# The minimum of 23 ELU blocks moves to GpSimd, and their relu passes go, in a fused attention and FFN kernel

## The chip, the core and the metric

The kernel runs on one core of a Trainium2 chip. The core has TensorE (PE, matmuls, with a queue for weight loads, PEld), VectorE (DVE), ScalarE (ACT), GpSimd (POOL) and SyncE (SP), which issues DMAs. Each engine works through its own instructions in the order in which the program gives them, and waits on semaphores for the others. GpSimd is used on SBUF alone in this kernel; PSUM is read by VectorE and ScalarE. The metric is the device time of one execution in microseconds. Two executions of the kernel before took 331.69 and 332.18 us, median 331.94 us.

## The reference

Attention over 8 batches, 8 heads, 576 queries and 16 "beacon" keys and values ahead of the 576 causal ones, head size 64; its output, 4608 tokens of 512 features, goes through an FFN with an ELU:

```python
scores = scale * np.matmul(q, k_all.transpose(0, 1, 3, 2))   # causal mask but for the beacons
a = np.exp(scores - scores.max(-1, keepdims=True)); a /= a.sum(-1, keepdims=True) + 1e-09
x = np.matmul(a, v_all)               # then to (4608, 512)
h = x @ w_in                          # 512 -> 2048
g = np.where(h > 0.0, h, 1.0 * (np.exp(np.minimum(h, 0.0)) - 1.0))
out = g @ w_out                       # 2048 -> 512
```

The inputs and the output are float32; the kernel works in 16-bit types with float32 sums.

## The kernel before

The tokens are cut into tiles, numbered 0 to 9: two of 256 tokens, then eight of 512. Attention runs by batch (0 to 7), the FFN by tile, interleaved. The whole program is one list of short words, written out by hand in several lines of text (the last argument of `run`); each word calls one step, and the order of the words is the order of the instructions on each engine. The tile framework adds the semaphores and takes buffers from pools in that same order. So a word may be moved only with all that it does on its engine.

The words that matter here, `t` being the tile and `i` a block of 512 PSUM columns:

- `F.t.i` (line 508): FFN1 of one block, four matmuls of 128x512 into a PSUM bank. The banks with the tag "hps" are two, and every F takes the older of them.
- `e.t.i` (line 518): ScalarE's exp of the bank into an SBUF tile "e" (float32, three buffers).
- `u.t.i` (line 524 on ScalarE; with `.v`, line 526 on VectorE): relu of the bank into an SBUF tile "r" (f16, three buffers).
- `k.t.i` (line 536): VectorE's min(exp - 1, relu) from the two SBUF tiles into the FFN2 operand "gt". For a positive h this is h, for a negative one exp(h) - 1.
- `r.t.i` (line 543) and `g.t.i` (line 548): the other form of the same ELU. `r` makes min(exp, 1) - 1 from the SBUF tile "e" into "r", and `g` takes max(h, r) with h read from the PSUM bank. There is no relu. The bank is released only by `g`.
- `Q.t.a.b` (line 624): steps a to b of the 112 matmuls of 128x256 of a tile's FFN2, a Strassen-like scheme of 7 phases of 16; `Z` (line 578) makes the sums of "gt" that it needs, `J` (lines 633 to 640) takes its results from PSUM (the ones on VectorE read PSUM and an SBUF tile) and stores them from SyncE's queue.
- `S`, `x`, `m`, `D`, `L`, `n`, `W`, `M`: a batch's scores (line 317), exp (332), causal mask on VectorE (337), partial sums of the exponentials on VectorE (390), row sums, their reciprocals on ScalarE, the product with v (374), and the scaling that makes the FFN's input (468).
- `P`, `K`, `E`, `U`, `V`, `X`, `H`: in tiles 8 and 9, 12 of the 16 blocks of FFN1 go through another Strassen-like scheme. `P` (line 694) are its matmuls, of 128x256, in the same two "hps" banks.
- `lk`, `lt`, `lp`, `lv`: loads; `lk` and `lv` are DMAs issued by GpSimd, `lp` are small copies on GpSimd.

In the kernel before eight blocks take the form `r`, `g`, with `r` on VectorE: seven in tile 6 and block 7.7. The others take `u` and `k`.

Of the kernel before, what the change touches and what calls it, by code (L numbers as in the profile page):

```python
# [17 lines left out]
def kernel(  # L18
# [519 lines left out]
    op["k"] = kk  # L538

    @step  # L540
    def r(t, i):
# [1 line left out]
        nc.vector.tensor_scalar(
            out=rb[t, i], in0=eb[t, i], scalar1=1.0, scalar2=1.0, op0=ALU.min, op1=ALU.subtract)

    @step
# [307 lines left out]
    m.5.3.1 F.5.10 x.6.8 F.5.5 D.5.3.1 Q.4.35.42 e.5.10 Q.4.42.49 u.5.5 J.4.2 S.6.9 S.6.10 e.5.5
    u.5.10.v k.5.10 Q.4.49.56 D.5.3.2 Z.4.4.1 x.6.10 F.5.8 u.5.8 D.5.2.0 Q.4.56.63 D.5.3.3 x.6.9
    F.5.3 m.6.1.0 S.6.6 Z.4.4.0 e.5.8 lt.7.0 x.6.6 D.5.2.1 k.5.14 D.5.2.2 W.5.1 D.5.2.3 k.5.8
    L.5.1 u.5.3 e.5.3 Q.4.63.70 lp.7.0 F.5.0 k.5.3 m.6.1.1 F.5.4 n.5.1 k.5.5 m.6.0.1 e.5.0
    Q.4.70.77 u.5.0 M.5.1.1 F.5.1 M.5.1.0 e.5.4 u.5.4 D.6.1.0 lp.7.1 J.4.3.v F.5.2 S.6.11 k.5.4
    S.6.12 D.6.0.0 u.5.1 Q.4.77.84 m.6.2.1 J.4.4 Q.4.84.91 e.5.1 k.5.1 D.6.0.1 x.6.12 x.6.11
    u.5.2 Q.4.91.98 D.6.1.1 S.7.4 k.5.0 S.7.2 e.5.2 Z.5.3.1 D.6.1.2 x.7.2 F.5.13 D.6.0.2 k.5.2  # L860
    D.6.1.3 Q.4.98.105 x.7.4 F.5.6 S.7.3 e.5.13 u.5.13 S.6.7 Q.4.105.112 u.5.6 x.7.3 e.5.6 x.6.7
    J.4.5 F.6.2 k.5.13 J.4.6.v e.6.2 D.6.0.3 u.6.2 W.6.0 lv.7 L.6.0 n.6.0 F.6.5 e.6.5 m.6.3.0
    k.5.6 m.6.2.0 u.6.5 m.6.3.1 Z.5.3.0 Z.5.1.0 F.6.3 e.6.3 u.6.3 D.6.2.0 Q.5.0.7 Q.5.7.14
    M.6.0.0 D.6.2.1 F.6.8 M.6.0.1 k.6.3 e.6.8 D.6.2.2 S.7.12 S.7.1 k.6.5 r.6.8 F.6.6 x.7.1
    x.7.12 e.6.6 g.6.8 Q.5.14.21 Z.5.1.1 Z.5.2.0 F.6.9 S.7.0 S.7.5 r.6.6 e.6.9 r.6.9 J.5.0 g.6.6
    D.6.3.0 D.6.2.3 g.6.9 x.7.0 k.6.2 m.7.0.0 Q.5.21.28 Q.5.28.35 J.5.1 x.7.5 F.6.0 Z.5.2.1
    S.7.11 D.6.3.1 u.6.0 e.6.0 S.7.6 F.6.13 F.6.14 D.6.3.2 x.7.6 W.6.1 e.6.13 x.7.11 r.6.13
    D.6.3.3 g.6.13 e.6.14 m.7.1.0 L.6.1 r.6.14 F.6.7 e.6.7 m.7.0.1 u.6.7 D.7.0.0 Q.5.35.42
    Q.5.42.49 F.6.12 D.7.0.1 n.6.1 g.6.14 e.6.12 M.6.1.1 u.6.12 F.6.10 Q.5.49.56 D.7.1.0 m.7.1.1
    J.5.2 k.6.12 F.6.1 M.6.1.0 k.6.0 Q.5.56.63 u.6.10 S.7.9 Z.5.4.1 S.7.8 Z.5.4.0 e.6.10  # L870
    Q.5.63.70 Q.5.70.77 e.6.1 x.7.8 r.6.1 F.6.4 k.6.7 J.5.3 e.6.4 g.6.1 Q.5.77.84 D.7.0.2 F.7.1
# [67 lines left out]
```

## Time and profile before

| | before |
|---|---|
| runs, median | 331.94 us (331.69 to 332.18) |
| profiled execution | 331.68 us |
| its span (first to last instruction) | 330.0 us |
| granted TensorE clock | 1.00 |
| TensorE busy | 98% |
| VectorE busy | 88% |
| ScalarE busy | 83% |
| GpSimd busy | 26% |

The page of a profile gives the busy time of each engine in the span of 330.0 us; the windows give the same for a stretch, with the count of instructions. A row of the groups names the line of the kernel, the engine, the operation, what it writes and reads, shapes, the count, then the busy time in us, the mean in ns of one, and the idle time just ahead of them with what ended it. A row of the timeline starts with the start and the length in us. A row of the waits says who waited for whom: us in total, times, the longest.

### The profile page before, as it was taken

The numbers are of one execution on the slowest core, as the hardware profiler recorded it, in microseconds if no ns is written. First come the engines' busy times: TensorE is split into PE (matmuls) and PEld (weight loads), VectorE is DVE, ScalarE is ACT, GpSimd is POOL, SyncE is SP. The second block draws the span as 40 slices with busy tenths as digits, with TensorE's granted clock in tenths as the row PEclk, the third lists the DMA queues.
The fourth block names the chain that finished last, engine by engine and source line by source line (L and its number), as shares of the span: only waits on it lengthen the run. The fifth ranks groups of instructions, "written<-read, shape, count | busy, mean of one in ns | idle before, by whom it ended". The sixth has DMA issues, their size and how long they took to land.

```text
span 330.0 us, 8747 instructions
## 1 busy us (share of the span) xinstructions
PE 321.8 (98%) x3576; PEld 209.5 (63%) x3576; DVE 291.2 (88%) x614; ACT 275.0 (83%) x446; POOL 85.0 (26%) x109
## 2 busy tenths in 40 slices
PE   8989999999999999999999999999999999999995
PEld 4657766444555656556566665556656888788884
DVE  3866897899899999999989999999998899999962
ACT  1999988999889988998999999878778787888730
POOL 8861659638317009103500230000000000000000
PEclk9999999999999999999999999999999999999999
DMA  9999799999999989998995591010200011010122
GB/s 118 170 178 204 105 191 171 166 154 175 144 147 176 173 98 116 151 135 118 124 149 108 101 105 65 2 34 18 79 3 33 33 66 34 32 66 32 35 97 96
DMA packets 130009, 34.65 MB, mean 105 GB/s; under 512 B 112816, under 2 KB 129456, under 8 KB 129968
## 3 DMA queue, kind: packets, MB, share of 16 engines
q0 software_dynamic: 95840, 18.49, 68.4%
q1 hardware_dynamic: 33408, 15.34, 24.0%
q8 instruction: 28, 0.46, 0.6%
q10 hardware_dynamic: 720, 0.26, 0.3%
q14 instruction: 13, 0.11, 0.1%
HBM read 37.22 MB, written 15.34 MB: 159 GB/s over the span
## 4 chain that ended last, share of the span: by engine, by line
PE 82%; ACT 11%; DVE 3%; issue 1%; DMA 1%; ACTq 0%; DVEq 0%
PE hps L508 28%; PE ops L624 25%; ACT et L332 7%; PE sc L317 6%; PE hps L694 6%; PE ut L374 6%; PE ops L557 4%; PE sx L624 2%; ACT e L518 2%; PE lt L374 2%; DMA lo<-in_beacon_k_dram 1%; ACT r L524 1%; DVE qk L390 1%; PE lt L416 1%; PE tp L263 1%
## 5 line engine op out<-in xcount | busy, mean ns | idle before, releaser
L508 PE MATMUL hps<-xT,w_in 128*128 128x512 f16 (+1 forms) x544 | 118.7, 355 | 0.5 <-DVE r L526 0.2
L332 ACT ACTIVATE et<-sc 128x1024 f16<-128x1024 f32 (+2 forms) x114 | 105.4, 988 | 11.4 <-PE sc L317 10.9
L624 PEld LDWEIGHTS <-gt 128*128 128x128 f16 x768 | 73.7, 98 | 19.2 <-issue 2.5
L518 ACT ACTIVATE e<-hps 128x512 f32<-128x512 f32 x120 | 72.6, 621 | 10.5 <-PE hps L508 7.1
L536 DVE SCALAR_TENSOR_TENSOR gt<-e,r 128x512 f16<-128x512 f32 x112 | 75.5, 684 | 4.2 <-ACT r L524 2.5
L508 PEld LDWEIGHTS <-w_in 128*128 128x128 f16 x544 | 50.1, 98 | 41.8 <-issue 5.1
L524 ACT ACTIVATE r<-hps 128x512 f16<-128x512 f32 x88 | 54.2, 623 | 6.6 <-PE hps L508 6.1
L624 PE MATMUL ops<-w_out,gt 128*128 128x256 f16 x368 | 47.9, 273 | 0.0
L624 PE MATMUL ops<-wt,gt 128*128 128x256 f16 x352 | 47.2, 273 | 0.0
L149 POOL DMA_DIRECT2D v<-in_v_dram x40 | 36.7, 1056 | 5.5 <-issue 4.4
L337 DVE TENSOR_TENSOR et<-et,triu 128x512 f16<-128x512 f16 (+4 forms) x108 | 31.7, 332 | 3.5 <-ACT et L332 3.5
L578 DVE TENSOR_TENSOR gt<-gt 128x1024 f16<-128x1024 f16 x48 | 32.0, 684 | 0.5
L390 DVE TENSOR_TENSOR qk<-qk,et 128x416 f16<-128x416 f16 (+2 forms) x66 | 23.7, 367 | 0.7
L374 PEld LDWEIGHTS <-v 128*32 128x32 f16 (+1 forms) x800 | 17.6, 96 | 10.2 <-issue 2.8
L144 POOL DMA_DIRECT2D v<-in_beacon_v_dram x8 | 6.8, 856 | 63.9 <-PE ops L624 25.5
L374 PE MATMUL ut<-et,v 128*32 128x464 f16 (+3 forms) x560 | 21.1, 296 | 0.0
L468 DVE TENSOR_TENSOR xT<-ut,rl 128x672 f16<-128x672 f32 (+12 forms) x26 | 16.5, 671 | 4.5 <-ACT rl L434 3.4
L526 DVE TENSOR_SCALAR r<-hps 128x512 f16<-128x512 f32 x24 | 16.4, 686 | 3.4 <-ACT e L518 3.3
L733 DVE SCALAR_TENSOR_TENSOR gt<-e,r 128x512 f16<-128x512 f32 x24 | 16.1, 685 | 0.6 <-ACT e L716 0.3
L640 DVE TENSOR_TENSOR osb<-ops,sm 128x512 f32<-128x512 f32 x23 | 15.7, 683 | 1.0 <-PE ops L624 1.0
L557 PE MATMUL ops<-w_out,gt 128*128 128x512 f16 x64 | 16.2, 380 | 0.0
L624 PE MATMUL ops<-w_out,s 128*128 128x256 f16 x112 | 15.0, 273 | 0.0
(113 smaller groups left out, 413.2 us busy)
## 6 DMA issues: line engine op xcount, KB each, us to landing
out_dram<-osb SPq DMA_DIRECT2D x35, 256.0 KB, 2.3
v<-in_v_dram POOLq DMA_DIRECT2D x24, 128.0 KB, 8.0
scr<-in_q_dram POOLq DMA_DIRECT2D x5, 576.0 KB, 14.6
scr<-in_k_dram POOLq DMA_DIRECT2D x5, 576.0 KB, 14.0
w_in<-in_moe_w_in_dram POOLq DMA_DIRECT2D x8, 256.0 KB, 9.0
w_out<-in_moe_w_out_dram POOLq DMA_DIRECT2D x4, 512.0 KB, 9.8
qst<-in_q_dram POOLq DMA_DIRECT2D x4, 288.0 KB, 5.9
kst<-in_k_dram POOLq DMA_DIRECT2D x4, 288.0 KB, 7.0
```

Of the source, the lines that this page charges most:

```text
L149: nc.gpsimd.dma_start(out=vt[b][r0:r0 + n, j, :, :], in_=v[b, :, ilo[j]:ilo[j] + n, :].rearrange("h s d -> s h d"),)
L332: nc.scalar.activation(out=ets[b, d][:, :, a - EC2 * d:e - EC2 * d], in_=sc[b, g][:, :, a - c0:e - c0], func=AFT.Exp, bias=0.0, scale=SCALE)
L337: nc.vector.tensor_tensor(out=o, in0=o, in1=i, op=ALU.mult)
L374: nc.tensor.matmul(out=t[32 * i:32 * (i + 1), a - qa:e - qa], lhsT=ones[0:kc[j], :] if half is None else v16[0:kc[j], j, h, half:D:2], rhs ...
L390: (nc.vector if eng == "v" else nc.gpsimd).tensor_tensor(out=o, in0=t[0:rows, :, a:e] if n == 0 else o, in1=t[0:rows, :, col:col + e - a], ...
L508: nc.tensor.matmul(out=h[:, n_, :], lhsT=w_in16[:, cc, P * fc:P * (fc + 1)], rhs=xt[k][:, cc, a - TT * k:e - TT * k], start=(cc == 0), sto ...
L518: nc.scalar.activation(out=eb[t, i], in_=flat(hp[t, i]), func=AFT.Exp, bias=0.0, scale=1.0)
L524: nc.scalar.activation(out=rb[t, i], in_=flat(hp[t, i]), func=AFT.Relu, bias=0.0, scale=1.0)
L536: nc.vector.scalar_tensor_tensor(out=half(t, i), in0=eb[t, i], scalar=1.0, in1=rb[t, i], op0=ALU.subtract, op1=ALU.min)
L557: nc.tensor.matmul(out=ob[t, tb_], lhsT=gt[:, fc, P * tb_:P * (tb_ + 1)], rhs=w_out16[:, fc, :], start=(fc == 0), stop=(fc == NFC - 1))
L578: (nc.vector if eng == "v" else nc.gpsimd).tensor_tensor(out=o_, in0=a_, in1=b_, op=op_)
L624: nc.tensor.matmul(out=xy[t, n_][:, qd, :], lhsT=lw[:, P * qd:P * (qd + 1)], rhs=wt_[:, c, :], start=(first and c == 0 and (qd == 0 or (t, ...
```

## The change

`r` can be told to run on GpSimd, and 23 blocks use it so: 15 of tile 7 (all but 7.1), and blocks 12 to 15 of tiles 8 and 9. Block 7.7 had `r` on VectorE before; the other 22 had `u` on ScalarE and `k` on VectorE, which become `r` on GpSimd and `g` on VectorE. From tile 5's last blocks on the words also stand in another order. No other word is added or removed. The code:

```diff
     @step
-    def r(t, i):
+    def r(t, i, eng="v"):
         rb[t, i] = melt.tile([P, 512], FP16, tag="r", name="r")
-        nc.vector.tensor_scalar(
+        (nc.gpsimd if eng == "p" else nc.vector).tensor_scalar(
             out=rb[t, i], in0=eb[t, i], scalar1=1.0, scalar2=1.0, op0=ALU.min, op1=ALU.subtract)
```

Of the order, tile 7's part:

```diff
...
-    r.6.11 g.6.11 Z.6.1.0 J.5.6 Z.6.1.1 F.7.6 D.7.3.0 e.7.6 k.7.12 m.7.2.0 F.7.2 D.7.3.1 D.7.2.0
-    D.7.2.1 u.7.6 k.7.6 D.7.3.2 e.7.2 Q.6.7.14 u.7.2 D.7.3.3 Q.6.14.21 F.7.15 Z.6.2.0 e.7.15
-    Q.6.21.28 u.7.15 D.7.2.2 n.7.0 F.7.7 k.7.1 F.7.8 k.7.15 e.7.7 J.6.0 M.7.0.0 r.7.7 e.7.8
-    D.7.2.3 g.7.7 u.7.8 k.7.8 W.7.1 L.7.1 F.7.13 u.7.13 e.7.13 F.7.5 Q.6.28.35 Z.6.4.0 F.7.0
...
+    u.7.1 D.7.0.2 Q.5.77.84 F.7.6 e.7.6 J.5.4 r.7.6.p Z.6.3.1 e.7.1 Q.5.84.91 Q.5.91.98 k.6.7
+    D.7.0.3 F.7.12 e.7.12 D.7.1.0 x.7.10 Q.5.98.105 Z.6.1.1 J.5.5 Q.5.105.112 S.7.9 g.7.6 x.7.9
+    S.7.7 F.7.2 S.7.12 m.7.1.1 r.7.12.p g.7.12 D.7.1.1 D.7.1.2 m.7.3.0 Z.6.3.0 F.7.14 e.7.2
+    Q.6.0.7 r.7.2.p x.7.12 D.7.1.3 g.7.2 Z.6.1.0 e.7.14 x.7.7 L.7.0 r.7.14.p m.7.3.1 g.7.14
+    F.7.15 m.7.2.0 e.7.15 J.5.6 r.7.15.p g.7.15 D.7.3.0 Q.6.7.14 S.7.8 x.7.8 F.7.8 D.7.2.0
+    m.7.2.1 Q.6.14.21 e.7.8 n.7.0 F.7.7 r.7.8.p g.7.8 Z.6.2.0 e.7.7 r.7.7.p k.7.1 W.7.1 F.7.5
+    e.7.5 g.7.7 r.7.5.p Z.6.2.1 J.6.0 Q.6.21.28 D.7.2.1 D.7.3.1 F.7.13 g.7.5 e.7.13 D.7.2.2
+    Q.6.28.35 r.7.13.p D.7.3.2 F.7.0 Q.6.35.42 M.7.0.0 g.7.13 J.6.1 D.7.3.3 e.7.0 D.7.2.3 F.7.10
+    L.7.1 r.7.0.p e.7.10 X.8.1 g.7.0 Q.6.42.49 Z.6.4.1 r.7.10.p g.7.10 F.7.4 J.6.2.v Q.6.56.63
+    n.7.1 e.7.4 F.7.3 e.7.3 Q.6.63.70 r.7.4.p M.7.1.0 r.7.3.p g.7.4 Z.6.4.0 Q.6.49.56 X.8.2
+    J.6.3 g.7.3 H.3.1 M.7.1.1 F.7.11 e.7.11 X.8.4 F.7.9 e.7.9 Q.6.70.77 Q.6.77.84 r.7.11.p
+    Q.6.84.91 g.7.11 r.7.9.p P.8.0.0 g.7.9 J.6.4 P.8.0.1 K.8.0.0 Q.6.91.98 K.8.0.1 H.3.0 P.8.0.2
...
+    Z.9.3.1 V.9.2.6 g.9.13 E.9.2.4 e.9.15 Q.8.105.112 J.8.6 Q.9.0.7 r.9.15.p Q.9.7.14 V.9.2.4
+    g.9.15 Z.9.2.0 Z.9.1.1 Q.9.14.21 J.9.0 Z.9.2.1 Q.9.21.28 Q.9.28.35 Q.9.35.42 J.9.1 Q.9.42.49
+    Q.9.49.56 J.9.2 Q.9.56.63 Q.9.63.70 J.9.3 Z.9.4.1 J.8.5 Z.9.4.0 Q.9.70.77 Q.9.77.84
...
```

More of the change, by code (lines that the diff above doesn't have):

```diff
@@ L854 @@
[L854 to L871, printed above, removed]
@@ new lines @@
+    P.8.1.6 U.8.1.6 E.8.1.6 Z.7.4.1 W.7.0 U.8.1.4 K.8.1.5 V.8.1.6 H.3.2 P.8.2.0 K.8.2.0 P.8.2.1
+    U.8.1.5 Q.7.35.42 P.8.2.2 J.7.1 K.8.2.1 K.8.2.2 V.8.1.1 Q.7.42.49 M.7.0.1 P.8.2.3 E.8.1.5
+    K.8.2.3 P.8.2.4 Q.7.49.56 K.8.2.4 V.8.1.5 E.8.2.1 P.8.2.5 U.8.2.1 P.8.2.6 E.8.2.6 K.8.2.5
+    Q.7.56.63 U.8.2.6 F.8.12 V.8.2.1 V.8.1.4 J.7.2.v e.8.12 F.8.14 U.8.2.5 Q.7.63.70 Q.7.70.77
+    X.9.1 J.7.3 X.9.2 Z.7.4.0 Q.7.77.84 r.8.12.p g.8.12 F.8.13 e.8.14 V.8.2.6 J.7.4 r.8.14.p
+    e.8.13 Q.7.84.91 r.8.13.p Q.7.91.98 g.8.14 U.8.2.4.v P.9.0.0 E.8.2.5 Q.7.98.105 X.9.4
@@ new lines @@
+    V.8.2.5 g.8.13 K.9.0.0 J.7.5 P.9.0.1 X.9.3 E.8.2.4 P.9.0.2 Q.7.105.112 K.9.0.1 K.9.0.2
+    P.9.0.3 Z.8.3.1 P.9.0.4 E.9.0.1 K.9.0.3 Q.8.0.7 P.9.0.5 V.8.2.4 K.9.0.4 U.9.0.1 U.9.0.4
+    J.7.6 P.9.0.6 Z.8.3.0 K.9.0.5 E.9.0.6 Q.8.7.14 P.9.1.0 U.9.0.5 K.9.1.0 Q.8.14.21 Q.8.21.28
+    V.9.0.1 U.9.0.6 E.9.0.4 J.8.0 E.9.0.5 P.9.1.1 Z.8.1.0 P.9.1.2 Z.8.1.1 Z.8.2.0 K.9.1.2
+    Z.8.2.1 K.9.1.1 Q.8.28.35 P.9.1.3 P.9.1.4 Q.8.35.42 V.9.0.5 K.9.1.3 U.9.1.1 J.8.1 E.9.1.1
+    K.9.1.4 V.9.0.6 P.9.1.5 P.9.1.6 K.9.1.5 V.9.0.4 Q.8.42.49 U.9.1.6 F.9.14 E.9.1.6 V.9.1.1
```

73 lines of the change are left out of this document (34 added, 39 removed).

## The prediction

> **What bounds the kernel now.** I read the profile's page first, for the share of each engine, then the windows, to see whether that share holds in the stages that the change touches, and then the waits.
>
> ```profile
> span 330.0 us, 8747 instructions
> ...
> PE 321.8 (98%) x3576; PEld 209.5 (63%) x3576; DVE 291.2 (88%) x614; ACT 275.0 (83%) x446; POOL 85.0 (26%) x109
> ```
>
> TensorE is at 98%, VectorE at 88%, ScalarE at 83%; GpSimd has most of its time free. Next come the windows of tile 7's FFN1 (234 to 257 us) and of tiles 8 and 9 (columns: stretch, length, then busy time and count by engine, the granted clock, DMA share and GB/s).
>
> ```profile
> 234.00:257.30 23.30, 23.30 (x196) 14.45 (x194) 21.90 (x47) 18.29 (x34) 0.00 (x0) 1.00 0.11 36
> 257.30:282.00 24.70, 24.70 (x246) 20.79 (x245) 23.31 (x42) 19.28 (x37) 0.00 (x0) 1.00 0.13 44
> 282.00:300.00 18.00, 18.00 (x154) 14.80 (x153) 17.09 (x31) 15.24 (x30) 0.00 (x0) 1.00 0.13 45
> 300.00:314.00 14.00, 14.00 (x119) 11.40 (x117) 13.02 (x23) 11.33 (x23) 0.00 (x0) 1.00 0.12 39
> ```
>
> TensorE is busy in every microsecond at the full granted clock; VectorE at 94%, 94%, 95% and 93%; GpSimd not at all; ScalarE is idle for 16 of the 80 us. A busy TensorE can still be slow, so I check its pace. The chain's rows give the pitch of an undisturbed stream; the next three rows count the matmuls from 265 to 312 us of line 508 (512 columns), line 624 and line 694 (256 columns each), and the last is what else ran there.
>
> ```profile
> 236.52 1.73 PE hps L508 x8
> ...
> 315.14 1.75 PE ops L624 x16
> ```
> ```profile
> 265.00:312.00 47.00, 7.82 (x32) 2.96 (x31) 1.00 0.13 45
> ...
> 265.00:312.00 47.00, 27.08 (x214) 20.84 (x214) 1.00 0.13 45
> ...
> 265.00:312.00 47.00, 18.72 (x140) 13.62 (x140) 1.00 0.13 45
> ...
> L374 PE MATMUL ut<-et,v 128*32 128x464 f16 (+3 forms) x40 | 1.5, 297 | 0.0
> ```
>
> 1.73/8 = 0.216 us for 512 columns and 1.75/16 = 0.109 us for 256. So 32 x 0.216 + (214 + 140) x 0.109 + 1.5 = 6.9 + 38.6 + 1.5 = 47.0 us of work in 47.0 us. There is nothing to win in this stretch except by giving TensorE less work, and the change gives it none less. In the waits from 200 us on, TensorE has a single row:
>
> ```profile
> PE hps L508 <- DVE gt L548: 0.2, 1, 0.2
> ```
>
> That one wait belongs to the form of block that the change makes more of.
>
> **The change part by part.** The two orders have the same 1505 steps except for the blocks named. What goes, and what comes in its place, by the groups:
>
> ```profile
> L536 DVE SCALAR_TENSOR_TENSOR gt<-e,r 128x512 f16<-128x512 f32 x112 | 75.5, 684 | 4.2 <-ACT r L524 2.5 <-ACT e L518 1.3
> ...
> L524 ACT ACTIVATE r<-hps 128x512 f16<-128x512 f32 x88 | 54.2, 623 | 6.6 <-PE hps L508 6.1 <-issue 0.2
> ...
> L548 DVE TENSOR_TENSOR gt<-hps,r 128x512 f16<-128x512 f32 x8 | 5.5, 684 | 0.1
> ...
> L543 DVE TENSOR_SCALAR r<-e 128x512 f16<-128x512 f32 x8 | 3.4, 421 | 0.2 <-ACT e L518 0.2
> ```
>
> *ScalarE* loses 22 relu passes (14 in tile 7, four each in tiles 8 and 9): 22 x 0.62 = 13.7 us. Beside a TensorE that waits 0.2 us, that is worth nothing in itself. *VectorE* swaps 22 times line 536 for line 548, 684 ns for 684 ns, and loses one line 543 (block 7.7): 0.4 us less. *TensorE* gets the same matmuls in another order from tile 5's last stage on. *DMAs* are the same; in GpSimd's queue all loads stand ahead of the first new pass, and the last v load is issued no later relative to its predecessors. Late in the order one VectorE sum with its store (tile 8, phase 5) now stands behind a step of tile 9's epilogue; it takes 0.68 us of a VectorE that is free by then. I put these at nothing; the cover is the closing run of matmuls of tile 9 (phases of 1.75 us).
>
> *GpSimd* gets 23 passes of 128x512 f32 from SBUF to f16. No row shows one. The nearest are a selection, which reads and writes SBUF (the row gives both its sizes), and small copies:
>
> ```profile
> L237 POOL TENSOR_SCALAR_AFFINE_SELECT triu<-triu x2: 306/353/400, 8.1 to 8.3; 128x128 f16<-128x128 f16 x1, 128x256 f16<-128x256 f16 x1
> ```
> ```profile
> 36.27 0.21 POOL L774 COPY qst<-bkT 128x32 bf16<-128x32 bf16 x1
> ```
> ```profile
> 131.89 1.29 DVE L578 TENSOR_TENSOR s<-gt 128x1024 f16<-128x1024 f16 x2
> ...
> 132.01 1.22 POOL L774 COPY kst<-bkT 128x32 bf16<-128x32 bf16 x1
> ```
>
> From 128 to 256 columns the selection grows by 94 ns, 0.73 ns a column, so 512 columns are 400 + 256 x 0.73 = 0.59 us. That is the low end. The same small copy takes 0.21 us with VectorE on small work and 1.22 us beside two back-to-back VectorE passes with both operands in SBUF: it waited 1.0 us. Low end plus that wait, 1.6 us, is the high end. I take **1.0 us**, nearer the low end: of VectorE's 21.9 us in the first window, 15 maxima x 0.684 = 10.3 us will read PSUM. The Trainium skill, "GPSIMD Engine Reference" (§3.1), gives 0.77 us for a 512-element loop of several operations on one GpSimd core. By that, as an estimate, the pass with the same allowance for waiting would be 1.2 us and the sum about 1.5 us longer; no row here shows it.
>
> What matters is the PSUM bank. FFN1 has two banks ("hps"). A relu block frees its bank when two ScalarE passes have read it. A changed block frees it only when VectorE's maximum is done, behind exp and behind GpSimd. So VectorE, busy at 94%, enters the loop that lets TensorE go on. Tile 6 has such blocks already, with the min pass on VectorE. The shortest (block 6.8) and the longest (6.14):
>
> ```profile
> 205.83 1.03 PE L508 MATMUL hps<-xT,w_in 128*128 128x512 f16 x4
> ...
> 207.07 0.60 ACT L518 ACTIVATE e<-hps 128x512 f32<-128x512 f32 x1 [1.07 <-DVE gt L536]
> ...
> 207.78 0.42 DVE L543 TENSOR_SCALAR r<-e 128x512 f16<-128x512 f32 x1
> ...
> 208.23 0.69 DVE L548 TENSOR_TENSOR gt<-hps,r 128x512 f16<-128x512 f32 x1
> ...
> 208.98 0.59 PE L508 MATMUL hps<-xT,w_in 128*128 128x512 f16 x2
> ```
> ```profile
> 213.96 1.46 PE L508 MATMUL hps<-xT,w_in 128*128 128x512 f16 x6
> ...
> 219.20 0.68 DVE L548 TENSOR_TENSOR gt<-hps,r 128x512 f16<-128x512 f32 x1
> ...
> 219.94 0.59 PE L508 MATMUL hps<-xT,w_in 128*128 128x512 f16 x2 [0.24 <-DVE gt L548]
> ```
>
> From the end of the block's matmuls to the end of the maximum: 208.92 - 206.86 = 2.06 us, and 219.88 - 215.42 = 4.46 us. Both times the next block on that bank starts 0.06 us behind the maximum. I call this the hold. On GpSimd 0.42 us becomes 1.0, and one more handoff is added, which I take as that from exp to min here (207.67 to 207.78), 0.1 us: 0.7 us more in all. The shortest hold becomes 2.75 us; the middle of the two (3.3) becomes 4.0.
>
> Against it stands the cover: the TensorE work between a block and the next that takes its bank. Example: between block 7.2 and block 7.15 the new order has one scores group, block 7.14, seven FFN2 matmuls and one row-sum group: 0.24 + 0.87 + 0.78 + 0.45 = 2.34 us, by the pitches above and, for scores and row sums, by their column counts at the same clock. Done so for 14 blocks of tile 7 from 7.12 on, in order: 3.1, 2.3, 3.1, 2.7, 3.1, 3.1, 2.4, 2.4, 2.9, 2.9, 3.2, 2.4, 3.2, 2.8; mean 2.83. Tile 8 and 9: 2.8, 3.2, 4.8, 2.8, 3.2, 3.6, and for the last two over 13.
>
> Which hold? While TensorE stands, VectorE's queue runs empty, so the hold can't stay at its long end: I take a third of the way from 2.75 to 4.0, **3.15 us**. With two banks in turn a shortfall is shared by two blocks: (3.15 - 2.83)/2 = 0.16 us x 14 = 2.2 us. In tiles 8 and 9 two blocks fall short by 0.35 us, sharing with Strassen groups that have none: 0.6 us in all. Sum: **+2.8 us**. The profiled execution took 331.68 us (span 330.0 and 1.7 around it): 331.68 + 2.8 = **334.5 us**. The median of the runs, 331.94, is 0.3 us above that execution, which I leave.
>
> Ends: at 1.6 us for the pass, with the shortest hold, 2.06 - 0.42 + 1.6 + 0.1 = 3.3 us, a little over what I take; at the middle hold with a pass of 1.0, 4.0 us, 0.58 x 14 = 8.2 plus about 2 in tiles 8 and 9, 342 us. Both long ends at once, 4.6 us, I leave out for the reason just given. At 0.59 us and the shortest hold, 2.06 - 0.42 + 0.59 + 0.1 = 2.33 us, every cover suffices: 331.7 us.
>
> Waits added: GpSimd waits for exp and for an "r" buffer (three of them, freed by the maximum); behind it are only its own later passes. VectorE's maximum waits for GpSimd, and behind it are the Z sums that FFN2 waits for and the D sums that the row sums wait for. ScalarE's exp waits for its "e" buffer three blocks back, now freed by GpSimd.
>
> **The rivals.**
>
> *Covered: 331.7 us.* The pass takes 0.6 us, runs while VectorE is on earlier work, and the covers hold. For: tile 6 has eight such blocks and TensorE waits 0.2 us. Against: four covers are 2.3 to 2.4 us, with no room for any queue.
>
> *Gain: 330.4 us.* The new order removes TensorE's small stops. The waits from 200 us on name those of its weight loads:
>
> ```profile
> PEld L317 <- issue: 1.7, 5, 0.4
> ...
> PEld L374 <- issue: 1.5, 4, 0.4
> ...
> PEld L508 <- issue: 0.8, 3, 0.4
> ...
> PEld L624 <- issue: 0.4, 2, 0.2
> ```
>
> 4.4 us in 14 stops, under each of which a matmul of up to 0.22 us still streams: 4.4 - 14 x 0.22 = 1.3 us that could go. Against: nothing that the change takes away stands in these rows.
>
> *VectorE and GpSimd shut each other out: 340.8 us.* VectorE passes with two SBUF operands (line 578, the D sums, the masks) and the new pass run one after the other. At 1.22 against 0.21 us above it was GpSimd that waited; a pass of 0.59 us that starts first makes VectorE wait in its turn, or VectorE stands at the maximum until the pass is through. If VectorE loses 0.59 us per block, tile 7 costs 15 x 0.59 - 1.4 (its idle time in the first window) = 7.5 us, and tiles 8 and 9 cost 8 x 0.59 - 3.3 (1.39 + 0.91 + 0.98) = 1.4 us: +8.9 us. It decides as soon as the loss per block passes 1.4/15 = 0.1 us. Against: the 10.3 us of maxima, with one operand in PSUM, leave the way free. The Trainium skill, "SBUF — State Buffer" (Who interferes with whom), states this as a rule: whichever of the two starts first holds a shared pair of ports for its whole instruction. The copy's 1.22 us agrees; that VectorE is the one who waits no run here shows.
>
> *The change doesn't do what it says:* GpSimd's passes could sit behind its loads. The last of these were issued at 188 us in the trace, 45 us ahead, so I give it no chance of its own.
>
> **How the numbers follow.** Forecast (333 to 338.6): 0.45. Covered: 0.25. Gain: 0.05. Shut out, with the forecast's long end (over 338.6): 0.25. The range of 331.0 to 341.0 leaves out half the gain and the upper part of the shut-out case, nearly 2 in 10. Two per cent, about what a measurement of this kernel can tell from no change, is 6.6 us. Faster by over 2% (under 325.3) has no case: 0.01. Slower by over 2% (over 338.6): 0.25. Within: 0.74.
>
> **What would show it.** Right: TensorE gets waits for line 548 in tile 7, 0.1 to 0.3 us a block; ScalarE's busy time falls by 13 to 14 us; GpSimd's new passes read 0.8 to 1.3 us; VectorE idles ahead of line 548, released by GpSimd. If passes read 0.6 us and TensorE has no waits, the covered case holds. If VectorE's Z and D sums grow or get gaps of over 0.3 us beside GpSimd, it is the shut-out. Most wrong would be a pass of over 1.6 us, or a TensorE that I counted as full and that wasn't.

## The result, and the profile after

The changed kernel takes 346.1 us (two runs, 345.92 and 346.27) against 331.94: 4.28% slower, with an interval of 4.02 to 4.53%. The forecast was 334.5 us with a range up to 341.0. The profiled execution took 346.27 us, with a span of 344.3.

The page of the kernel after answers the first rows of before: TensorE's share falls from 98 to 95% and GpSimd's busy time grows by 45.5 us. Its row of slices (8.6 us each) dips from about 240 us on and at the end.

```profile
span 344.3 us, 8769 instructions
...
PE 325.7 (95%) x3576; PEld 209.6 (61%) x3576; DVE 295.3 (86%) x613; ACT 266.4 (77%) x424; POOL 130.5 (38%) x132
...
PE   8979999999999999999999999999887999898985
PEclk9999999999999999999999999999999999999988
...
PE 67%; ACT 12%; POOL 10%; DVE 5%; issue 3%; DMA 1%; POOLq 1%; ACTq 0%; DVEq 0%
```

The last row is the chain that ended last, by engine: the new GpSimd pass has 10% of it. In the span, 14.3 us were added. TensorE's idle time rose from 330.0 - 321.8 = 8.2 to 344.3 - 325.7 = 18.6 us, so 10.4 of them are TensorE standing still; its busy time rose by 3.9 us with the same 3576 matmuls. The windows of the kernel after (same columns as in the prediction) show where it stands:

```profile
230.00:265.00 35.00, 30.86 (x269) 18.92 (x268) 28.69 (x58) 18.07 (x28) 28.47 (x15) 1.00 0.09 31
265.00:289.00 24.00, 22.27 (x220) 18.19 (x219) 21.82 (x39) 16.34 (x30) 2.86 (x2) 1.00 0.14 46
289.00:309.00 20.00, 18.44 (x159) 15.36 (x158) 17.87 (x32) 13.59 (x26) 6.03 (x3) 1.00 0.16 53
309.00:322.00 13.00, 12.10 (x98) 9.38 (x97) 10.96 (x19) 10.07 (x19) 3.87 (x2) 1.00 0.06 21
322.00:330.00 8.00, 6.04 (x46) 4.41 (x45) 5.92 (x9) 2.67 (x5) 4.59 (x2) 0.93 0.10 33
```

Of the 10.4 us, 4.1 go in tile 7's stage (35.00 - 30.86), 1.7 + 1.6 + 0.9 in those of tiles 8 and 9, and 2.0 in the eight microseconds around the last block. The waits from 200 us on name one cause for nearly all of it (who waited for whom, us, times, longest):

```profile
DVE gt L548 <- POOL r L543: 12.2, 17, 1.8
...
ACT e L518 <- POOL r L543: 4.4, 3, 1.8
PE hps L508 <- DVE gt L548: 4.2, 8, 1.0
PE hps L694 <- DVE gt L548: 3.8, 6, 0.9
...
PE ops L624 <- DVE gt L548: 1.8, 1, 1.8
```

TensorE waits for line 548, the maximum: 4.2 + 3.8 us for a PSUM bank and 1.8 us for the data of the last block, 9.8 us in all where the kernel before had 0.2. One step back, VectorE waits 12.2 us at that maximum for GpSimd. The instructions behind it, from the answer about line 543 (minimum, median and maximum in ns, then first and last start) and from the groups:

```profile
L543 POOL TENSOR_SCALAR r<-e x23: 1912/1918/2390, 230.9 to 325.6; 128x512 f16<-128x512 f32 x23
...
L543 DVE TENSOR_SCALAR r<-e x7: 410/421/427, 204.6 to 227.6; 128x512 f16<-128x512 f32 x7
```
```profile
L548 DVE TENSOR_TENSOR gt<-hps,r 128x512 f16<-128x512 f32 x30 | 20.7, 690 | 12.8 <-POOL r L543 12.2
L524 ACT ACTIVATE r<-hps 128x512 f16<-128x512 f32 x66 | 41.3, 632 | 3.6 <-PE hps L508 2.9 <-DVE gt L548 0.4
```

**A pass takes GpSimd 1.92 us at the median and never less than 1.91**, 4.6 times VectorE's 0.42 for the same operation on the same shapes. The prediction took 1.0 and had 1.6 as its high end.

A block of tile 7 shows what that does to the bank. The rows are from the timeline (start and length in us):

```profile
239.28 1.02 PE L508 MATMUL hps<-xT,w_in 128*128 128x512 f16 x4 [0.48 <-DVE gt L548]
...
240.41 0.60 ACT L518 ACTIVATE e<-hps 128x512 f32<-128x512 f32 x1 [1.80 <-POOL r L543]
...
241.08 2.14 POOL L543 TENSOR_SCALAR r<-e 128x512 f16<-128x512 f32 x1 [0.69 <-ACT e L518]
```
```profile
243.26 0.69 DVE L548 TENSOR_TENSOR gt<-hps,r 128x512 f16<-128x512 f32 x1 [1.81 <-POOL r L543]
...
244.00 1.02 PE L508 MATMUL hps<-xT,w_in 128*128 128x512 f16 x4 [0.88 <-DVE gt L548]
```

From the end of the block's matmuls (239.28 + 1.02 = 240.30) to the end of the maximum (243.95) are 3.65 us, and the next block starts 0.05 us later, after TensorE has stood for 0.88. Hardly any queue is in this hold: exp starts 0.11 us after the matmuls, GpSimd 0.07 after exp, the maximum 0.04 after GpSimd. (The 1.80 us that exp waits for GpSimd are for an "e" buffer; that pass ends at 240.39, only 0.09 us after the block's matmuls.)

### The profile page after: what moved, and what is told of

The parts are those of the page before. It is cut to its first block, busy times and chain, and to the rows that moved or that the text cites. A ratio compares the mean times of both kernels' runs of the same rounds, so it can differ in the third digit from the quotient of the medians.

```text
span 344.3 us, 8769 instructions
## 1 busy us (share of the span) xinstructions
PE 325.7 (95%) x3576; PEld 209.6 (61%) x3576; DVE 295.3 (86%) x613; ACT 266.4 (77%) x424; POOL 130.5 (38%) x132
## 4 chain that ended last, share of the span: by engine, by line
PE 67%; ACT 12%; POOL 10%; DVE 5%; issue 3%; DMA 1%; POOLq 1%; ACTq 0%; DVEq 0%
PE hps L508 23%; PE ops L624 18%; POOL r L543 10%; ACT et L332 7%; PE sc L317 6%; PE ut L374 5%; PE hps L694 5%; PE ops L557 4%; ACT e L518 3%; DVE gt L548 2%; PE sx L624 2%; PE lt L374 2%; DVE gt L733 1%; DMA lo<-in_beacon_k_dram 1%; ACT r L524 1%
## 5 line engine op out<-in xcount | busy, mean ns | idle before, releaser
L624 PEld LDWEIGHTS <-gt 128*128 128x128 f16 x768 | 74.5, 99 | 23.0 <-issue 2.7
L543 POOL TENSOR_SCALAR r<-e 128x512 f16<-128x512 f32 x23 | 45.8, 1997 | 85.3 <-ACT e L518 75.1
L536 DVE SCALAR_TENSOR_TENSOR gt<-e,r 128x512 f16<-128x512 f32 x90 | 60.4, 683 | 2.8 <-ACT r L524 1.6
L624 PE MATMUL ops<-w_out,gt 128*128 128x256 f16 x368 | 49.1, 276 | 2.0 <-DVE gt L548 1.8
L524 ACT ACTIVATE r<-hps 128x512 f16<-128x512 f32 x66 | 41.3, 632 | 3.6 <-PE hps L508 2.9
L578 DVE TENSOR_TENSOR gt<-gt 128x1024 f16<-128x1024 f16 x48 | 32.8, 696 | 0.4
L548 DVE TENSOR_TENSOR gt<-hps,r 128x512 f16<-128x512 f32 x30 | 20.7, 690 | 12.8 <-POOL r L543 12.2
L390 DVE TENSOR_TENSOR qk<-qk,et 128x672 f16<-128x672 f16 (+2 forms) x66 | 23.6, 373 | 0.7
L704 ACT COPY kst<-hps 128x512 f32<-128x512 f32 x18 | 10.5, 587 | 10.7 <-PE hps L694 10.3
L733 DVE SCALAR_TENSOR_TENSOR gt<-e,r 128x512 f16<-128x512 f32 x24 | 16.6, 700 | 0.1
```

The costliest lines, as they stand in the source:

```text
L524: nc.scalar.activation(out=rb[t, i], in_=flat(hp[t, i]), func=AFT.Relu, bias=0.0, scale=1.0)
L536: nc.vector.scalar_tensor_tensor(out=half(t, i), in0=eb[t, i], scalar=1.0, in1=rb[t, i], op0=ALU.subtract, op1=ALU.min)
L543: (nc.gpsimd if eng == "p" else nc.vector).tensor_scalar(out=rb[t, i], in0=eb[t, i], scalar1=1.0, scalar2=1.0, op0=ALU.min, op1=ALU.subtract)
L548: nc.vector.tensor_tensor(out=half(t, i), in0=flat(hp[t, i]), in1=rb[t, i], op=ALU.max)
L578: (nc.vector if eng == "v" else nc.gpsimd).tensor_tensor(out=o_, in0=a_, in1=b_, op=op_)
L624: nc.tensor.matmul(out=xy[t, n_][:, qd, :], lhsT=lw[:, P * qd:P * (qd + 1)], rhs=wt_[:, c, :], start=(first and c == 0 and (qd == 0 or (t, ...
```

## The experiments

Each is compared with the kernel before on the same chip (331.9 to 332.2 us). Steps that stand in more than one block are shown by one of them.

**The order alone** (e1_order_only). All 23 blocks go back to relu and the fused minimum; the relu stands where GpSimd's pass stood.

```diff
-    S.7.7 F.7.2 S.7.12 m.7.1.1 r.7.12.p g.7.12 D.7.1.1 D.7.1.2 m.7.3.0 Z.6.3.0 F.7.14 e.7.2
+    S.7.7 F.7.2 S.7.12 m.7.1.1 u.7.12 k.7.12 D.7.1.1 D.7.1.2 m.7.3.0 Z.6.3.0 F.7.14 e.7.2
```

> The changed order kept word for word, but the 23 blocks go back to their old form (relu on ScalarE in the place of the GpSimd pass, min(exp - 1, relu) on VectorE in the place of the maximum). Theory H (the GpSimd pass of 1.9 us holds the PSUM bank and TensorE stands) and theory X (VectorE and GpSimd shut each other out): 331 to 334 us, no waits of TensorE for line 548 in tile 7. Theory O (the new order itself costs the time): 340 us or more.

Measured: 335.17 us, +0.83% [0.59, 1.08], so some 3 us over the kernel before and over the 331 to 334 that were expected. But this kernel had a cost of its own in the waits from 200 us on: VectorE stands for the relu, which comes late in ScalarE's queue (0.7 us of such waits in before).

```profile
DVE gt L536 <- ACT r L524: 5.2, 6, 2.0
```

**The order alone, with the relu directly behind exp** (e11_order_relu_first) takes that cost out; against the last kernel:

```diff
-    D.7.0.3 F.7.12 e.7.12 D.7.1.0 x.7.10 Q.5.98.105 Z.6.1.1 J.5.5 Q.5.105.112 S.7.9 k.7.6 x.7.9
-    S.7.7 F.7.2 S.7.12 m.7.1.1 u.7.12 k.7.12 D.7.1.1 D.7.1.2 m.7.3.0 Z.6.3.0 F.7.14 e.7.2
+    D.7.0.3 F.7.12 e.7.12 u.7.12 D.7.1.0 x.7.10 Q.5.98.105 Z.6.1.1 J.5.5 Q.5.105.112 S.7.9 k.7.6 x.7.9
+    S.7.7 F.7.2 S.7.12 m.7.1.1 k.7.12 D.7.1.1 D.7.1.2 m.7.3.0 Z.6.3.0 F.7.14 e.7.2 u.7.2
```

> As e1 (the changed order, no GpSimd passes), but ScalarE makes the relu directly behind exp and not at the place where the GpSimd pass stood. e1 took 335.2 us, 3 us over before, and VectorE waited 5.2 us for relus there. If the late relus are the 3 us: 331.5 to 333 us, so that the order itself costs nothing. If the order of the other steps costs them: 335 us again.

Measured: 333.40 us, +0.43% [0.15, 0.71]. VectorE's wait for the relu falls from 5.2 to 2.2 us:

```profile
DVE gt L536 <- ACT r L524: 2.2, 5, 0.7
```

So the new order costs about 1.2 us by itself (0.5 to 2.4 by the interval), where 333 us at most were expected if the late relus were all, and about 3 where the relu stands late; the rest of the 14.2 us belongs to the new form of the blocks, with its pass on GpSimd.

**The pass on VectorE** (e2_min_on_dve): the changed kernel, order and all, without the `.p`.

```diff
-    S.7.7 F.7.2 S.7.12 m.7.1.1 r.7.12.p g.7.12 D.7.1.1 D.7.1.2 m.7.3.0 Z.6.3.0 F.7.14 e.7.2
+    S.7.7 F.7.2 S.7.12 m.7.1.1 r.7.12 g.7.12 D.7.1.1 D.7.1.2 m.7.3.0 Z.6.3.0 F.7.14 e.7.2
```

> The changed kernel with the 23 min passes on VectorE at 0.42 us instead of GpSimd at 1.9 us; form and order kept, no work for GpSimd. VectorE gets 9.7 us more, 6.3 of them in tile 7, where it had about 1.4 us free. Theory H: the hold is as short as in tile 6, what is left is VectorE's load: 334 to 338 us. Theory X: the same, as nothing is shut out. Theory O: 340 us or more.

Measured: 339.37 us, +2.07% [1.66, 2.48], more than the 334 to 338 us that were expected. VectorE, with 23 passes more than the changed kernel's, is now nearly full in tile 7's stage (third busy time in the row):

```profile
230.00:265.00 35.00, 32.21 (x283) 20.19 (x281) 33.11 (x76) 18.64 (x29) 0.00 (x0) 1.00 0.09 31
```

So the relu-free form without GpSimd costs 7.4 us, the order's share included, and with the same passes on the idle engine it costs nearly twice that. Freeing VectorE of 23 x 0.42 = 9.7 us is what GpSimd was to do, and it costs more than it frees.

**What a GpSimd pass costs, by its kind** (e8_pass_prices): the kernel before, with eight kinds of passes, three times each, that nobody reads, behind GpSimd's last loads (`ts` is minimum and subtract, or with False the minimum alone; d and s are where it writes and reads, 16 and 32 the bits).

```diff
+for _ in range(3):
+    ts(d16, s32, 512, True)
+    ts(d16, s32, 512, False)
+    ts(d16, s32, 256, True)
+    ts(d16, s16, 512, True)
+    ts(d16, s16, 512, False)
+    ts(d32, s32, 256, True)
+    nc.gpsimd.tensor_copy(out=d16, in_=s32)
+    nc.gpsimd.tensor_tensor(out=d16, in0=s16, in1=s16, op=ALU.add)
```

> The kernel before, with GpSimd passes that nobody reads put behind the last v load (about 192 us), three rounds of eight kinds on 128 rows: min and subtract from f32 to f16 at 512 and 256 columns, min alone, the same two from f16, f32 to f32 at 256 columns, a copy f32 to f16, and a sum of two f16 operands. If the price is per column: 256 columns at 1.0 us. If it is in the arithmetic: min alone at 1.0 to 1.3 us, the copy below that. If it is in the float32 input: f16 at about 1.0 us. If it was waiting for VectorE: values far apart from round to round, with a low one at 0.6 to 1.0 us. The time itself: 332 to 334 us.

Measured in the third round, by groups (the rounds before have longer passes among them; each of the first two rows holds the two-op and the one-op pass, 2.00 and 2.00 us from f16, 1.97 and 1.49 from f32; the row of the sum takes in one of the second round):

```profile
L548 POOL TENSOR_SCALAR bkT<-wt 128x512 f16<-128x512 f16 x2 | 4.0, 2004 | 0.2
L548 POOL TENSOR_SCALAR bkT<-wt 128x512 f16<-128x512 f32 x2 | 3.5, 1731 | 0.2
L559 POOL TENSOR_TENSOR bkT<-wt 128x512 f16<-128x512 f16 x2 | 2.1, 1065 | 0.2
L548 POOL TENSOR_SCALAR bkT<-wt 128x256 f32<-128x256 f32 x1 | 1.1, 1117 | 0.1
L548 POOL TENSOR_SCALAR bkT<-wt 128x256 f16<-128x256 f32 x1 | 1.1, 1069 | 0.1
L558 POOL CAST bkT<-wt 128x512 f16<-128x512 f32 x1 | 0.6, 609 | 0.1
```

A copy of 512 columns takes 0.61 us, which is what the prediction's extrapolation (0.59) gives. The operation with two constants takes three times that. Between 256 columns here and 512 in after it grows by (1.92 - 1.07)/256 = 3.3 ns a column; the selection, from which the prediction drew its price, grew by 0.73. Reading f16 instead of f32 saves nothing: over the three rounds the least time with either input is 1.92 to 1.97 us for two operations and 1.49 for one, so leaving the second operation out saves about a quarter. The time of this kernel, in its one run, was 336.91 us, against 332 to 334 expected: passes that nobody reads cost some 5 us.

**The same framework with a cheap pass** (e14_copy_pass): the changed kernel with a plain copy on GpSimd in the pass's place. The minimum and the subtraction are left out in these 23 blocks, so they compute max(h, exp h).

```diff
+if eng == "p":
+    nc.gpsimd.tensor_copy(out=rb[t, i], in_=eb[t, i])
+    return
```

> The changed kernel with the GpSimd pass as a plain copy f32 to f16, 0.61 us in e8; min and subtraction are left out, so the kernel computes max(h, exp(h)) in these blocks. This is about the price that the prediction built on (0.59 us alone, 1.0 with waiting). If the price was the step that failed: 333 to 337 us, with VectorE's wait for GpSimd under 4 us. If GpSimd in this loop costs whatever its price: 341 us or more.

Measured: 335.07 us, +0.84% [0.59, 1.08], which is 11 us less than with the real pass, at the same order, the same handoffs, the same buffers and the same missing relus. The group of the pass, and tile 7's window:

```profile
L544 POOL CAST r<-e 128x512 f16<-128x512 f32 x23 | 17.8, 775 | 102.6 <-ACT e L518 87.4 <-DVE gt L736 8.3 <-DVE qk L390 2.5
```
```profile
230.00:265.00 35.00, 34.00 (x305) 22.46 (x304) 32.29 (x66) 20.06 (x33) 11.74 (x15) 1.00 0.12 39
```

```profile
DVE gt L551 <- POOL r L544: 1.5, 3, 0.5
```

With a mean pass of 0.78 us TensorE is busy for 34.0 of 35.0 us again, and VectorE's wait for GpSimd falls from 12.2 to 1.5 us. The length of the pass is what decides.

**A shorter pass that still computes the ELU** (e5_one_op): GpSimd makes min(exp, 1) only, VectorE's last step subtracts 1 and takes the maximum in one instruction.

```diff
+nc.gpsimd.tensor_scalar(out=rb[t, i], in0=eb[t, i], scalar1=1.0, scalar2=None, op0=ALU.min)
...
+nc.vector.scalar_tensor_tensor(
+    out=half(t, i), in0=rb[t, i], scalar=1.0, in1=flat(hp[t, i]), op0=ALU.subtract, op1=ALU.max)
```

> The changed kernel, with the GpSimd pass cut to one operation, min(exp, 1), and the subtraction moved into VectorE's maximum, which becomes (r - 1) max h at the same 684 ns. Theory V: the wait shrinks with the pass; if min alone takes 1.2 us, 23 x 0.7 us less wait, 338 to 341 us; if the pass stays at 1.9 us, 346 us.

Measured: 339.94 us, +2.45% [2.16, 2.75]. The pass's mean falls from 2.00 to 1.58 us:

```profile
L547 POOL TENSOR_SCALAR r<-e 128x512 f16<-128x512 f32 x23 | 36.2, 1578 | 89.3 <-ACT e L518 78.5 <-DVE gt L743 7.6 <-DVE qk L390 1.6
```

23 x 0.42 = 9.7 us less of GpSimd bring 6.2 us of time. With e14 (0.78 us) and after (2.00 us) that makes three points: 335.1, 339.9 and 346.1 us. Per microsecond of pass the kernel loses 4.9/0.80 = 6 us between the first two and 6.2/0.42 = 15 between the last two: the longer the pass, the less is hidden. (VectorE's last step is as long as in after, a median of 686 ns against 692.)

**Tile 7 alone and tiles 8 and 9 alone** (e3_tile7, e4_tiles89): the blocks of the other stage go back to relu as in the first experiment.

```diff
-    e.9.14 U.9.1.5.v Z.8.4.0 r.9.14.p V.9.1.6 F.9.12 g.9.14 e.9.12 Q.8.56.63 r.9.12.p Q.8.49.56
+    e.9.14 U.9.1.5.v Z.8.4.0 u.9.14 V.9.1.6 F.9.12 k.9.14 e.9.12 Q.8.56.63 u.9.12 Q.8.49.56
```
```diff
-    S.7.7 F.7.2 S.7.12 m.7.1.1 r.7.12.p g.7.12 D.7.1.1 D.7.1.2 m.7.3.0 Z.6.3.0 F.7.14 e.7.2
+    S.7.7 F.7.2 S.7.12 m.7.1.1 u.7.12 k.7.12 D.7.1.1 D.7.1.2 m.7.3.0 Z.6.3.0 F.7.14 e.7.2
```

> The changed order, with only the 15 blocks of tile 7 in the GpSimd form; tiles 8 and 9 as in e1. If the costs of the stages add up: e1 plus what the changed kernel has over e4, 335.2 + (346.1 - 340.8) = 340.5 us. Theory V or H: 340 to 341 us. If GpSimd's passes in tile 7 cost what their length says (15 x 1.2 us over a VectorE pass plus waits): 345 us or more.

> The changed order, with only the eight blocks of tiles 8 and 9 in the GpSimd form; tile 7 as in e1. GpSimd has 8 x 1.95 = 16 us of work in some 70 us. Theory H: each block still stops TensorE, and the last one does so ahead of tile 9's closing matmuls: 337 to 340 us. Theory T (GpSimd is short of time: 15 passes of 1.95 us in a stage of 27 us): 332 to 334 us, as there is time to spare here.

Measured: 340.26 us (+2.43% [2.0, 2.85]), as expected, and 340.76 us (+2.73% [2.03, 3.43]), a little over the 337 to 340 expected. With the shared order taken out once, 8.1 + 8.8 - 3.2 = 13.7 us, against 14.2 measured for both: the stages add up, as far as intervals of 2.8 and 4.6 us can tell. Eight blocks in tiles 8 and 9 cost as much as 15 in tile 7, though GpSimd is busy there for a small part of the time. The group of the pass in the kernel with tiles 8 and 9 alone, its first and last start (last two times of the row), and two rows of its waits:

```profile
L543 POOL TENSOR_SCALAR r<-e 128x512 f16<-128x512 f32 x8 | 16.6, 2087 | 109.7 <-ACT e L518 101.2 <-DVE gt L733 7.7 <-DVE gt L548 0.9
```
```profile
L543 POOL TENSOR_SCALAR r<-e x8: 1913/2042/2389, 268.3 to 320.6; 128x512 f16<-128x512 f32 x8
```
```profile
PE hps L694 <- DVE gt L548: 3.0, 5, 0.9
...
PE ops L624 <- DVE gt L548: 1.8, 1, 1.8
```

16.6 us of passes lie between 268 and 323 us. There GpSimd's throughput can't be the limit; it is the delay of the single block that TensorE pays, 3.0 us for banks and 1.8 for the last block.

**The last two blocks back** (e10_last_two_back).

```diff
-    F.9.13 V.9.2.1 Q.8.98.105 E.9.2.5 E.9.2.6 U.9.2.5.v V.9.2.5 F.9.15 Z.9.1.0 e.9.13 r.9.13.p
-    Z.9.3.1 V.9.2.6 g.9.13 E.9.2.4 e.9.15 Q.8.105.112 J.8.6 Q.9.0.7 r.9.15.p Q.9.7.14 V.9.2.4
-    g.9.15 Z.9.2.0 Z.9.1.1 Q.9.14.21 J.9.0 Z.9.2.1 Q.9.21.28 Q.9.28.35 Q.9.35.42 J.9.1 Q.9.42.49
+    F.9.13 V.9.2.1 Q.8.98.105 E.9.2.5 E.9.2.6 U.9.2.5.v V.9.2.5 F.9.15 Z.9.1.0 e.9.13 u.9.13
+    Z.9.3.1 V.9.2.6 k.9.13 E.9.2.4 e.9.15 Q.8.105.112 J.8.6 Q.9.0.7 u.9.15 Q.9.7.14 V.9.2.4
+    k.9.15 Z.9.2.0 Z.9.1.1 Q.9.14.21 J.9.0 Z.9.2.1 Q.9.21.28 Q.9.28.35 Q.9.35.42 J.9.1 Q.9.42.49
```

> The changed kernel with only the last two blocks (9.13 and 9.15) back in the relu form. In the changed kernel TensorE stood 1.8 to 2.0 us ahead of tile 9's closing matmuls for the last of them, and then ran at half the granted clock for 3.4 us (1.7 us lost). If the two are the cause: 342 to 343 us, no stop of over 0.5 us there and no half clock before the end. If they only show what VectorE is late by anyway: 345 us or more.

Measured: 343.51 us, 2.6 less than the changed kernel and a little over the 342 to 343 expected. The timeline of after shows the stop, and its windows the granted clock behind it (the column behind the busy times):

```profile
328.03 0.69 DVE L548 TENSOR_TENSOR gt<-hps,r 128x512 f16<-128x512 f32 x1 [1.81 <-POOL r L543]
...
328.78 2.00 PE L624 MATMUL ops<-w_out,gt 128*128 128x256 f16 x9 [1.80 <-DVE gt L548]
```
```profile
324.00:328.80 4.80, 2.85 (x26) 2.15 (x24) 2.80 (x6) 1.59 (x3) 3.29 (x2) 1.00 0.16 55
328.80:332.40 3.60, 3.60 (x18) 2.53 (x19) 3.35 (x6) 0.00 (x0) 0.00 (x0) 0.53 0.01 2
332.40:336.00 3.60, 3.60 (x35) 3.22 (x34) 0.96 (x2) 1.17 (x2) 0.00 (x0) 1.00 0.45 150
```

FFN2 of the last tile needs the last block's data; with nothing else left to do TensorE stands for 1.8 us. Then it runs at a granted clock of 0.53 for 3.6 us: 18 matmuls where the next 3.6 us hold 35. In the run with the two blocks back that wait is gone, and the window from 322 to 336 us shows a clock of 1.00 throughout. 1.8 + 1.7 = 3.5 us were there to win, 2.6 came; a wait of 0.4 us for a Z sum is new there. The stop alone doesn't bring the low clock: the kernel with tiles 8 and 9 alone has the same wait of 1.8 us, until 323.8 us, and a clock of 1.00 behind it:

```profile
324.00:326.00 2.00, 1.60 (x15) 1.19 (x14) 1.90 (x4) 0.00 (x0) 0.00 (x0) 1.00 0.00 0
326.00:328.00 2.00, 2.00 (x20) 1.79 (x19) 2.00 (x4) 0.59 (x1) 0.00 (x0) 1.00 0.37 125
```

**GpSimd's passes without a reader** (e7_no_reader): the kernel before, its order unchanged, with 23 passes of the same operation behind the 23 blocks' last steps (they read its result, in f16); nobody reads what they make.

```diff
+    def y(t, i):
+        nc.gpsimd.tensor_scalar(
+            out=bkT.bitcast(FP16).rearrange("p a b -> p (a b)"), in0=half(t, i), scalar1=1.0, scalar2=1.0, op0=ALU.min, op1=ALU.subtract)
...
-    r.6.11 g.6.11 Z.6.1.0 J.5.6 Z.6.1.1 F.7.6 D.7.3.0 e.7.6 k.7.12 m.7.2.0 F.7.2 D.7.3.1 D.7.2.0
+    r.6.11 g.6.11 Z.6.1.0 J.5.6 Z.6.1.1 F.7.6 D.7.3.0 e.7.6 k.7.12 y.7.12 m.7.2.0 F.7.2 D.7.3.1 D.7.2.0
```

> The kernel before, with 23 GpSimd passes of the same form (f16 input) behind the last VectorE step of the same 23 blocks; they read the finished block and write to a tile that nobody reads, so only the shared SBUF side is tested. Theory X (VectorE's and GpSimd's passes shut each other out and that is the cost): VectorE's passes with two SBUF operands grow by 3 us or more in all, as in the changed kernel (where they grew by about 3 us), and the time is 335 us or more. Theory V (VectorE stands at a block's last step until GpSimd is through, and has no time to spare): no such standing here; 332 to 334 us.

Measured: 335.34 us, +0.97% [0.74, 1.2]: 3.4 us with no bank held and no one waiting for a result; one Z sum, which writes over what a pass reads, waits 0.5 us for it. What is left is that both engines use SBUF. Some of VectorE's passes with both operands in SBUF grow; in before no Z sum exceeds 694 ns. First, from this kernel's answer about the line of the Z sums (583 here), the row of most of them; then the same from after:

```profile
L583 DVE TENSOR_TENSOR gt<-gt x48: 676/684/1100, 97.8 to 322.2; 128x1024 f16<-128x1024 f16 x48
```
```profile
L578 DVE TENSOR_TENSOR gt<-gt x48: 675/683/1096, 97.6 to 332.7; 128x1024 f16<-128x1024 f16 x48
L578 DVE TENSOR_TENSOR s<-gt x16: 675/682/1102, 72.6 to 323.0; 128x1024 f16<-128x1024 f16 x16
```

Summed over VectorE's passes, the growth over the usual length of each is 3.5 us in 11 passes here and 3.2 us in 9 passes in after. VectorE has little to spare, and TensorE waits for what it makes. The maxima, which read one operand from PSUM, don't grow (677 to 692 ns for all 30 of after). In e14, beside the copies, VectorE's passes grow by as much, some 3 to 4 us, though that kernel is only 2.9 us over before. So this growth isn't what makes the changed kernel 11 us longer than e14, and how much of e7's 3.4 us it explains isn't settled.

**Free the bank early** (e6_sum_form): relu stands directly behind exp, so that ScalarE frees the bank as in before; GpSimd works in place on the exp tile, and VectorE adds the two SBUF tiles.

```diff
-    D.7.0.3 F.7.12 e.7.12 D.7.1.0 x.7.10 Q.5.98.105 Z.6.1.1 J.5.5 Q.5.105.112 S.7.9 g.7.6 x.7.9
-    S.7.7 F.7.2 S.7.12 m.7.1.1 r.7.12.p g.7.12 D.7.1.1 D.7.1.2 m.7.3.0 Z.6.3.0 F.7.14 e.7.2
+    D.7.0.3 F.7.12 e.7.12 u.7.12 D.7.1.0 x.7.10 Q.5.98.105 Z.6.1.1 J.5.5 Q.5.105.112 S.7.9 a.7.6 x.7.9
+    S.7.7 F.7.2 S.7.12 m.7.1.1 r.7.12.p a.7.12 D.7.1.1 D.7.1.2 m.7.3.0 Z.6.3.0 F.7.14 e.7.2 u.7.2
...
+    def a(t, i):
+        nc.vector.tensor_tensor(out=half(t, i), in0=eb[t, i], in1=rb[t, i], op=ALU.add)
```

> The changed order and the 23 GpSimd passes kept, but the bank is freed early: ScalarE makes the relu again just behind exp, GpSimd writes min(exp, 1) - 1 over the exp tile, and VectorE adds the two from SBUF (684 ns, as the maximum). The result is the same ELU. Theory H: TensorE no longer waits for VectorE's last step except at the end of tile 9; 333 to 337 us. Theory T: GpSimd's 29 us in tile 7 still set the pace: 338 us or more. Theory X: GpSimd's passes still lengthen VectorE's, more than before as the sum reads SBUF twice: 338 us or more.

Measured: 346.61 us, the same as the changed kernel. The bank is free, and VectorE stands at the sum in its place:

```profile
DVE gt L556 <- POOL e L543: 10.6, 12, 1.8
```

And TensorE stands for what is queued behind it, here the partial sums of the exponentials:

```profile
PE lt L416 <- DVE qk L390: 2.6, 1, 2.6
```

The 333 to 337 us expected of a free bank did not come: VectorE, full as it is, can't stand for 10 us either. The experiment isn't clean, as the sums read both operands from SBUF and grow beside GpSimd, five of the 23 from 0.69 to about 1.1 us; VectorE's growth is some 6 us here against 3 in after. So it doesn't show that the held bank is worth nothing.

**Take VectorE's standing away as well** (e12_sum_later): as the last one, with tile 7's sums one block later in VectorE's order.

```diff
-    S.7.7 F.7.2 S.7.12 m.7.1.1 r.7.12.p a.7.12 D.7.1.1 D.7.1.2 m.7.3.0 Z.6.3.0 F.7.14 e.7.2 u.7.2
-    Q.6.0.7 r.7.2.p x.7.12 D.7.1.3 a.7.2 Z.6.1.0 e.7.14 u.7.14 x.7.7 L.7.0 r.7.14.p m.7.3.1 a.7.14
+    S.7.7 F.7.2 S.7.12 m.7.1.1 r.7.12.p a.7.6 D.7.1.1 D.7.1.2 m.7.3.0 Z.6.3.0 F.7.14 e.7.2 u.7.2
+    Q.6.0.7 r.7.2.p x.7.12 D.7.1.3 a.7.12 Z.6.1.0 e.7.14 u.7.14 x.7.7 L.7.0 r.7.14.p m.7.3.1 a.7.2
```

> As e6 (bank freed early, GpSimd's pass written over the exp tile, sum on VectorE), but in tile 7 each sum stands one block later in VectorE's order, about 2 us, so that VectorE need not stand for GpSimd. Theory V (VectorE's standing is the cost): its wait for GpSimd, 10.6 us in e6, falls by half, and the time from 346.6 to 340 to 342 us. Theory T (GpSimd's 15 passes of 2 us set tile 7's pace): 345 us or more.

Measured: 344.80 us, 1.8 less, and not the 340 to 342 us expected if VectorE's standing were all. Now GpSimd is late by itself: a row of its timeline has nine passes back to back, and the row below, from the chain that ended last, has the same nine.

```profile
246.79 20.96 POOL L543 TENSOR_SCALAR e<-e 128x512 f32<-128x512 f32 x9 [0.49 <-ACT e L518]
```
```profile
246.79 20.98 POOL e L543 x9
```

20.96/9 = 2.33 us a pass, beside sums with both operands in SBUF, and VectorE still waits 9.0 us for it. In tile 7 the bank, VectorE's queue and GpSimd's own throughput (15 passes of 1.92 us are 28.8 us, in a stage that took 27 in the kernel before) are all short in these kernels, and with the short pass of e14 hardly any of them is. Relieving one brings the next.

No kernel here is faster than the one before; the nearest is the new order with relu, 333.40 us.

## Why the prediction was wrong, by its steps

- **TensorE is the bound, and taking ScalarE's relus away is worth nothing: right.** In e14 they are gone, and the time is 335.07 us against 333.40 with them in the same order. Line 524's group fell from 54.2 to 41.3 us, 12.9 of the 13.7 foreseen. The page's busy time fell only from 275.0 to 266.4, short of "13 to 14": its groups add up every pass's own length (over all of ScalarE's groups, 312 us in before and 299 after), while the busy share counts overlapping passes once.
- **VectorE's swap of line 536 for 548, 684 ns each: right** (690 ns).
- **The price of GpSimd's pass: the step that failed.** "I take 1.0 us", between 0.59 and 1.6; measured 1.92 at the least crowded and 2.00 in the mean. The low end was drawn from a selection and holds for a copy (0.61); it doesn't hold for an operation with two constants. The high end added only a wait for the ports to that low end, so both ends stood on the wrong kind of operation. The prediction named it: "Most wrong would be a pass of over 1.6 us". The Trainium skill, "GPSIMD Engine Reference" (§3.1), gives 0.77 us for a 512-element loop, and its §4.1 calls one-input work there about line rate. The measurement, 1.92 us against VectorE's 0.42, differs from both and decides.
- **The hold of the bank: right in form.** The prediction's shortest hold with 1.92 in the place of 1.0 is 2.06 - 0.42 + 1.92 + 0.1 = 3.66 us; the block shown has 3.65. Its taken hold becomes 3.15 + 0.92 = 4.07, and 14 x (4.07 - 2.83)/2 = 8.7 us in tile 7 by the prediction's own sum. That is too much: e3 measured 8.1 over before, but 1.2 (e11) to 3.2 us (e1) of that are the order and late relus, which leaves 4.9 to 6.9. The shortest hold gives 14 x (3.66 - 2.83)/2 = 5.8. That it fits in size is partly luck, since in e6, with the bank free, VectorE's standing and its longer sums cost as much.
- **The new order "at nothing": wrong by about 1.2 us** (e11), without a single wait that names it.
- **The last two blocks, with "over 13" us of cover: wrong.** That cover counted only who takes the bank next. Whoever reads the block's data waits too, and FFN2 of the last tile had nothing else to do: 2.6 us by e10, the half clock behind the stop included.
- **Rivals.** "Shut out" (0.25, 340.8 us) is real, but small: 3.4 us in e7, where nothing else of the change is there. The Trainium skill, "SBUF — State Buffer" (Who interferes with whom), says that the one that starts first blocks the other for its whole instruction; that VectorE waits too is now shown, by up to 0.42 us a pass in after (1102 ns against 682) and 0.86 in e8 (line 536, 1547 against 685), not by a whole pass of 1.92. The rival's second half, VectorE standing at the maximum "until the pass is through", is the larger: 12.2 us of waiting, priced at 0.59 where the pass takes 1.92. "Covered" would have needed a pass of 0.6 us, and even the copy in e14 (0.78 in the mean) costs 3 us. "Gain" fell with e11, where the order alone is slower.

With the copy the change comes out at 335.07, half a microsecond from the forecast, but that is partly luck: the copy's 0.78 us is shorter than the 1.0 taken, and 1.2 of its 2.9 us are the order, which the forecast had at nothing. On the line from e14 to e5, 6 us per microsecond of pass, a pass of 1.0 us would give about 336.4 us (an estimate): inside the range, and above the forecast by little more than the order. What remains open is how the 11 us above the copy divide between bank, VectorE and GpSimd; in e6 and e12 they take each other's place, so a sum of three terms isn't to be had. About 2 us of TensorE's longer busy time (3.9 less 1.7 for the half clock) are in no wait. An estimate accounts for them: where a stream stops, its last matmul shows its whole length (the block's row of four has 1.02 us, 4 x 0.216 = 0.86 by the pitch), and 15 stops at line 548 make 15 x 0.16 = 2.4 us. A version with the maximum one block later, bank and all, wasn't tried: there are two banks, and the block after next needs the one that it would keep.
